# Attention with the values as stationary columns, one stream of scores in threes, and a hand-written order of side work

## The chip, the cores and the metric

The kernel runs on one NeuronCore of a Trainium2 chip. The core has five engines that run side by side and wait for each other by semaphores: TensorE (PE, matmuls; PEld is its weight load), VectorE (DVE), ScalarE (ACT, here the exponentials), GpSimd (POOL) and SyncE (SP, which issues the DMAs). The metric is the device time of one execution in microseconds, as the median of several runs. A profile is one further execution, whose span goes from its first to its last instruction.

## What is computed

Two branches on the same `x` (2048 tokens, 448 features, bf16), mixed by a gate per token. Branch A is attention with 16 heads of 28 features; branch B is a filter in the frequency domain.

```python
qkv = (x @ wqkv).reshape(B, S, 3, H, Dh)...        # S = 2048, H = 16, Dh = 28
p = softmax(einsum("bhqd,bhkd->bhqk", q, k) * Dh ** -0.5)
a = einsum("bhqk,bhkd->bhqd", p, v)...  @ wo
X = rfft2(x) * (w_r + 1j * w_i)
b = irfft2(X)
g = sigmoid((x * gate_w).sum(-1, keepdims=True))
out = g * a + (1 - g) * b
```

The Fourier transforms are matmuls with constant matrices, in several stages: along the features (f1), then along the tokens in two steps (stage A, and f34, which also multiplies by the filter), then back (stage A again as f5, and f678).

## The kernel before

**Head.** `phase_setup` loads `x` as one DMA, transposes it on TensorE (64 transposes, L257) into `xT`, and prepares weights. `proj_setup`, `proj_matmuls` (L353), `proj_knorm` and `proj_qbias` build q and k for head 15 (copied to three row groups by DMA, L359) and for the first four heads; `vproj_and_gate` (L290) makes all values `vsb`, with a column of ones beside each head, and the gate. Then the main loop starts.

**Softmax without a maximum.** Each query and key carries one extra row, so that a score comes out with a bound subtracted: half the squared query norm and half the largest squared key norm. The exponential can then follow the scores directly.

**Main loop.** `main_loop_group` takes heads in groups: first head 15 alone with three query blocks of 512 (and then its fourth block alone, the 16 narrow exponentials), then five groups of three heads. For each block of 128 keys it computes three score tiles of 128 keys by 512 queries in row groups of the array (L553), one exponential over the three (L557, `Pt`), and twelve small matmuls (L562) in which 128 columns of `Pt` are the weights and the 29 columns of `vsb` move. `psPV` collects queries on partitions, so the denominator is a column: after 16 key blocks VectorE takes the reciprocal of 12 columns (L568) and multiplies three times into `osb` (L571).

**Side work.** The projections of the other heads (`proj_tile`) and the Fourier stages (L603 to L718) are written after the groups with a lower priority; the scheduler of the framework places them where engines have room. They share one PSUM buffer, `ps_bg`; the scores have two buffers of three banks each, and `psPV` has one. `tail` transposes `osb`, multiplies by `wo` (L747), applies gate and branch B (L749) and stores (L751).

Of the kernel before, what the change touches and what calls it, by code (L numbers as in the profile page):

```python
# [17 lines left out]
BG_PRIORITY_BASE = 10_000_000  # L18


def bcast_last(ap: bass.AP, n: int) -> bass.AP:
    assert ap.ap[-1][1] == 1
    new_ap = [list(p) for p in ap.ap[:-1]] + [[0, n]]
    return bass.AP(tensor=ap.tensor, offset=ap.offset, ap=new_ap)


def strided_rows(t_ap: bass.AP, row0: int, stride: int, count: int) -> bass.AP:
    pstep = t_ap.ap[0][0]
    return _AP(tensor=t_ap.tensor, offset=t_ap.offset + row0 * pstep,
               ap=[[pstep * stride, count]] + [list(x) for x in t_ap.ap[1:]])  # L30


def chunks_of(n: int, c: int):
    return [(i, min(c, n - i)) for i in range(0, n, c)]


def fft_consts(S: int, D: int):
    NT = S // 128
    P = 128
    J = P // NT  # L40
    F = D // 2 + 1
    F2 = 2 * F
    bf16 = ml_dtypes.bfloat16
    fch = chunks_of(F, 128)
# [4 lines left out]
    dch = chunks_of(D, 128)  # L49
    Bd_pad = np.zeros((len(dch) * 128, F2))  # L50
    Bd_pad[:D] = Bd
    c["Bd"] = np.ascontiguousarray(Bd_pad.reshape(len(dch), 128, F2).transpose(1, 0, 2))
# [3 lines left out]
    Es = np.sin(2 * np.pi * pp * bb / P)  # L56
    def perm(M):
        return np.ascontiguousarray(M.reshape(P, J, NT).transpose(0, 2, 1).reshape(P, P))
# [34 lines left out]
    Binv = np.zeros((P, 2 * len(fch), D))  # L93
    qi = 0
    for B in (Br, Bi):
        for (fs, fn) in fch:
            Binv[:fn, qi, :] = B[fs:fs + fn, :]
            qi += 1
    c["Binv"] = Binv
    return {k: v.astype(np.float32).astype(bf16) for k, v in c.items()}  # L100


class Kernel:
    def __init__(self, tc, A_x, A_wqkv, A_wo, B_w_r, B_w_i, gate_w, out):
        self.tc = tc
        nc = self.nc = tc.nc
        self.A_x, self.A_wqkv, self.A_wo = A_x, A_wqkv, A_wo
        self.B_w_r, self.B_w_i, self.gate_w, self.out_ap = B_w_r, B_w_i, gate_w, out
        self.H = H = 16
        self.S = S = A_x.shape[1]  # L110
        self.D = D = A_x.shape[2]
        self.Dh = Dh = D // H
        self.SCALE = float(Dh) ** -0.5
        self.NT = NT = S // 128
        self.P = P = 128
        self.J = P // NT
        self.F = F = D // 2 + 1
        self.F2 = 2 * F
        self.dch = chunks_of(D, 128)
        self.NDC = len(self.dch)  # L120
        self.fch = chunks_of(F, 128)
        self.QW = 512
        assert Dh + 1 <= 32 and S % 512 == 0 and P % NT == 0 and NT <= P and H % 4 == 0
        self.x = A_x[0]
        self.outv = out[0].rearrange("(p t) d -> p t d", t=NT)
        self.tiles = [[(s, 4 * T + s) for s in range(4)] for T in range(H // 4)]
        lastT = len(self.tiles) - 1
        hl = H - 1
        self.tiles[lastT] = [(s, h) for (s, h) in self.tiles[lastT] if h != hl]
        self.tiles.append([(0, hl)])  # L130
        self.repT = len(self.tiles) - 1
        self.head_loc = {}
        for T, ent in enumerate(self.tiles[:-1]):
            for s, h in ent:
                self.head_loc[h] = (T, s)
        groups = [("rep", hl)]
        others = [h for h in range(H) if h != hl]
        for i in range(0, len(others), 3):
            groups.append(("tri", others[i:i + 3]))
        self.groups = groups  # L140
        self.NG = len(groups)
        self._bgcount = 0
        self._bg_saved = None
        self._evac_cnt = 0

    def bg_begin(self):
        assert self._bg_saved is None
        self._bg_saved = self.tc.cur_priority
        self.tc.cur_priority = BG_PRIORITY_BASE + self._bgcount

    def bg_end(self):
        assert self._bg_saved is not None
        self._bgcount = self.tc.cur_priority - BG_PRIORITY_BASE
        self.tc.cur_priority = self._bg_saved
        self._bg_saved = None

    def setup_pools(self, ctx):
        tc = self.tc
        self.per = ctx.enter_context(tc.tile_pool(name="per", bufs=1))
        self.rot2 = ctx.enter_context(tc.tile_pool(name="rot2", bufs=2))  # L160
        self.rot3 = ctx.enter_context(tc.tile_pool(name="rot3", bufs=3))
        self.ps = ctx.enter_context(tc.tile_pool(name="ps", bufs=2, space=bass.MemoryType.PSUM))
# [10 lines left out]
    def evac2(self, o, i):  # L173
        if self._evac_cnt % 2 == 0:
            self.nc.vector.tensor_copy(out=o, in_=i)
        else:
            self.nc.scalar.copy(out=o, in_=i)
        self._evac_cnt += 1

    def build(self):  # L180
        with ExitStack() as ctx:
            self.setup_pools(ctx)
            self.phase_setup()
            self.fft_setup()
            NTL = len(self.tiles)
            self.qTt = [None] * NTL
            self.kTt = [None] * NTL
            def full_proj(Tlist):
                for T in Tlist:
                    self.proj_setup(T)  # L190
                for which in ("q", "k"):
                    for T in Tlist:
                        self.proj_matmuls(T, which)
                for T in Tlist:
                    self.proj_knorm(T)
                for T in Tlist:
                    self.proj_qbias(T)
            full_proj([self.repT, 0])
            self.vproj_and_gate()
            bg_items = [("proj", T) for T in range(1, NTL - 1)]  # L200
            bg_items += [("fft", f) for f in
                         [self.fft_f1, self.fft_f2, self.fft_f34, self.fft_f5, self.fft_f678]]
            npj = NTL - 2
            plan = {0: [0, npj], 1: [1, npj + 1], 2: [2, npj + 2], 3: [npj + 3], 4: [npj + 4]}
            issued = set()
            for g in range(self.NG):
                self.main_loop_group(g)
                self.bg_begin()
                for idx in plan.get(g, []):
                    if idx < len(bg_items) and idx not in issued:  # L210
                        kind, arg = bg_items[idx]
                        if kind == "proj":
                            self.proj_tile(arg, bg=True)
                        else:
                            arg()
                        issued.add(idx)
                self.bg_end()
            self.bg_begin()
            for idx in range(len(bg_items)):
                if idx not in issued:  # L220
                    kind, arg = bg_items[idx]
                    if kind == "proj":
                        self.proj_tile(arg, bg=True)
                    else:
                        arg()
                    issued.add(idx)
            self.tail()
            self.bg_end()

    def phase_setup(self):  # L230
        nc = self.nc
        P, NT, D, S, NDC, H, Dh = self.P, self.NT, self.D, self.S, self.NDC, self.H, self.Dh
        per = self.per
        dch = self.dch
        self.xtok = per.tile([P, NT, D], BF16, name="xtok", tag="xtok_osb")
        nc.sync.dma_start(out=self.xtok[:], in_=self.x.rearrange("(p t) d -> p t d", t=NT))
        self.ident = per.tile([P, P], BF16, name="ident")
        make_identity(nc, self.ident[:])
        W3 = 3 * D + 1
        self.Wqkv_sb = per.tile([P, NDC, W3], BF16, name="Wqkv_sb")  # L240
        self.Wo_sb = per.tile([P, NDC, D], BF16, name="Wo_sb")
        for c, (d0, dsz) in enumerate(dch):
            nc.sync.dma_start(out=self.Wqkv_sb[0:dsz, c, 0:3 * D], in_=self.A_wqkv[d0:d0 + dsz, :])
        for c, (d0, dsz) in enumerate(dch):
            nc.sync.dma_start(out=self.Wqkv_sb[0:dsz, c, 3 * D:3 * D + 1],
                              in_=self.gate_w[d0:d0 + dsz].rearrange("(d o) -> d o", o=1))
        for c, (d0, dsz) in enumerate(dch):
            nc.sync.dma_start(out=self.Wo_sb[0:dsz, c, :], in_=self.A_wo[d0:d0 + dsz, :])
        self.xT = per.tile([P, NDC, S], BF16, name="xT")
        TB = 12  # L250
# [550 lines left out]
```

## Time and profile before

| | us |
|---|---|
| three runs | 572.0, 582.96, 583.14 |
| median | 582.96 |
| span of the profiled execution | 564.9 |
| first wide exponential starts | 56.8 |
| last exponential ends | 545.4 |

```profile
## 2 busy tenths in 40 slices
PE   2979988999998899999899999999998998899986
...
ACT  2153986999999899999899999999999999999961
...
PEclk9989985699999575799575555757799589999996
```

The page divides the span into 40 equal slices, and each digit is the busy share of a slice in tenths. PEclk is the clock that TensorE was granted, in tenths of full speed. After the first four slices TensorE and ScalarE are both busy for nearly all of the span; the clock changes between about 5 and 9. A group of instructions is given with its line, engine, shapes, count, busy time and mean duration, and then the idle time of its engine just before it with what ended it. In a table of stretches, the columns behind the five engines' busy times are granted clock, DMA share and GB/s.

### The profile page before, as it was taken

To read this page: it belongs to the slowest core of one execution; us is meant where nothing else is said; L and a number is where in the kernel's file an instruction comes from. 1 tells how busy PE (TensorE), PEld (TensorE's weight loads), DVE (VectorE), ACT (ScalarE), POOL (GpSimd) and SP (SyncE) were. 2 spreads that over 40 slices of the span, in tenths; PEclk is the share of its full clock that TensorE was granted. 3 is DMA by queue.
4 is the path that set the end of the run, shared out by engine and by line. 5 is a ranking of instruction groups with operands and counts; after the bars stand their busy time and mean duration, and the time that the engine had idled before them with its cause. 6 is when DMAs were issued, how large, how long until landed. Compare 5 with 4: busy or idle time off the path is not lost.

```text
span 564.9 us, 13975 instructions
## 1 busy us (share of the span) xinstructions
PE 508.8 (90%) x6088; PEld 256.5 (45%) x6088; DVE 213.8 (38%) x633; ACT 490.0 (87%) x392; POOL 20.8 (4%) x92
## 2 busy tenths in 40 slices
PE   2979988999998899999899999999998998899986
PEld 2424432444443355544355555555544554445541
DVE  4573323322223533322556555333233233333343
ACT  2153986999999899999899999999999999999961
POOL 6240010000000000000000000000000000000000
PEclk9989985699999575799575555757799589999996
DMA  7300000000000000000012221000000000000111
GB/s 252 126 19 20 2 2 1 2 1 2 2 1 2 3 1 1 1 3 1 1 33 54 55 55 26 1 2 1 20 21 20 21 20 20 21 1 27 34 34 41
DMA packets 13947, 13.45 MB, mean 24 GB/s; under 512 B 6191, under 2 KB 12783, under 8 KB 13758
## 3 DMA queue, kind: packets, MB, share of 16 engines
q1 hardware_dynamic: 13886, 12.57, 7.8%
q8 instruction: 47, 0.77, 0.6%
q14 instruction: 14, 0.11, 0.1%
HBM read 10.14 MB, written 1.84 MB: 21 GB/s over the span
## 4 chain that ended last, share of the span: by engine, by line
ACT 48%; PE 39%; issue 7%; DVE 3%; DMA 1%; SPq 0%; ACTq 0%
ACT Pt L557 48%; PE psS L553 12%; PE psPV L562 9%; PE pv L290 2%; PE pqk L353 2%; PE psT L641 2%; DMA Wqkv_sb<-in_A_wqkv_dram 1%; PE psY L714 1%; PE pf_s L747 1%; PE ptx L257 1%; PE psB L662 1%; PE psA L623 1%; PE psZ L705 1%; DVE fin L749 1%; PE psB L664 1%
## 5 line engine op out<-in xcount | busy, mean ns | idle before, releaser
L557 ACT ACTIVATE Pt<-psS 128x1536 bf16<-128x1536 f32 (+1 forms) x352 | 469.4, 1460 | 19.4 <-PE psS L553 10.2
L562 PEld LDWEIGHTS <-Pt 128*128 128x128 bf16 x4096 | 142.3, 100 | 131.1 <-ACT Pt L557 109.6
L562 PE MATMUL psPV<-vsb,Pt 128*128 128x29 bf16 x4096 | 167.1, 182 | 25.3 <-ACT Pt L557 20.8
L553 PE MATMUL psS<-qTa_2343,kTa_2344 32*128 32x512 bf16 x256 | 69.3, 507 | 0.5 <-ACT Pt L557 0.5
L553 PE MATMUL psS<-qTa_950,kTa_951 32*128 32x512 bf16 x256 | 68.8, 530 | 0.4 <-ACT Pt L557 0.4
L553 PE MATMUL psS<-qTa_249,kTa_250 32*128 32x512 bf16 x256 | 60.6, 439 | 1.8 <-ACT Pt L557 1.8
L553 PE MATMUL psS<-qTa_3760,kTa_3761 32*128 32x512 bf16 x192 | 26.5, 384 | 0.5 <-ACT Pt L557 0.4
L718 DVE TENSOR_SCALAR bm_sb<-psY,omg 128x448 bf16<-128x448 f32 x16 | 10.9, 683 | 36.8 <-PE psY L714 36.8
L667 DVE CAST Xri<-psB 128x225 bf16<-128x225 f32 x16 | 6.3, 396 | 25.7 <-PE psB L665 25.7
L749 DVE SCALAR_TENSOR_TENSOR fin<-pf,gsb,bm_sb 128x448 bf16<-128x448 f32 x12 | 8.2, 684 | 20.7 <-PE pf L747 20.7
L257 PE MATMUL ptx<-ident,xtok 128*128 128x128 bf16 (+1 forms) x64 | 6.7, 287 | 10.3 <-DMA xtok<-in_A_x_dram 7.7
L553 PEld LDWEIGHTS <-kTa_250 32*128 32x128 bf16 x256 | 12.8, 93 | 6.4 <-issue 2.3
L747 PE MATMUL pf<-Wo_sb,oTt 128*128 128x448 bf16 (+1 forms) x48 | 14.8, 374 | 0.7 <-DVE oTt L740 0.7
L553 PE MATMUL psS<-qTa_207,kTa_208 32*128 32x512 bf16 x64 | 14.4, 420 | 0.6 <-ACT Pt L557 0.5
L553 PEld LDWEIGHTS <-kTa_951 32*128 32x128 bf16 x256 | 13.0, 97 | 4.1 <-issue 1.8
L553 PEld LDWEIGHTS <-kTa_2344 32*128 32x128 bf16 x256 | 13.0, 95 | 3.6 <-issue 1.2
L571 DVE TENSOR_TENSOR osb<-psPV,recip 128x112 bf16<-128x112 f32 x64 | 13.6, 266 | 0.6
L290 PE MATMUL pv<-Wqkv_sb,xT 128*128 128x449 bf16 x64 | 13.5, 372 | 0.0
L603 DVE CAST V_5523<-psA 97x256 bf16<-97x256 f32 x16 | 6.8, 424 | 16.4 <-PE psA L625 16.4
L603 DVE CAST U_192<-psA 128x256 bf16<-128x256 f32 x16 | 6.8, 425 | 15.7 <-PE psA L625 15.7
L623 PE MATMUL psA<-R_sb,X_sb 128*128 128x256 bf16 (+1 forms) x32 | 12.2, 383 | 0.0
L623 PE MATMUL psA<-R_sb,G_sb 128*128 128x256 bf16 (+1 forms) x32 | 12.2, 382 | 0.0
(484 smaller groups left out, 541.6 us busy)
## 6 DMA issues: line engine op xcount, KB each, us to landing
RBg<-cRB SPq DMA_DIRECT2D x16, 128.0 KB, 2.0
xtok<-in_A_x_dram SPq DMA_DIRECT2D x1, 1792.0 KB
out_dram<-fin SPq DMA_DIRECT2D x16, 112.0 KB, 1.7
CSg<-cCS SPq DMA_DIRECT2D x16, 96.0 KB, 1.8
Wqkv_sb<-in_A_wqkv_dram SPq DMA_DIRECT2D x3, 336.0 KB, 7.4
Wg<-in_B_w_r_dram SPq DMA_DIRECT2D x16, 56.2 KB, 1.8
Wg<-in_B_w_i_dram SPq DMA_DIRECT2D x16, 56.2 KB, 2.0
Bd_sb<-cBd SPq DMA_DIRECT2D x1, 450.0 KB, 3.8
```

The source lines that it names most:

```text
L257: nc.tensor.transpose(out=pt[0:dsz, k, :], in_=self.xtok[:, t, d0:d0 + dsz], identity=self.ident[:])
L290: nc.tensor.matmul(pv[:, e, 0:D + 1], lhsT=self.xT[:, c, 128 * t:128 * t + 128], rhs=self.Wqkv_sb[:, c, 2 * D:3 * D + 1], start=(c == 0), ...
L353: nc.tensor.matmul(pqk[0:M, e, :], lhsT=Wg[:, c, 0:M], rhs=self.xT[:, c, 512 * b:512 * b + 512], start=(c == 0), stop=(c == NDC - 1))
L553: nc.tensor.matmul(psS[:, e, :], lhsT=kTa[32 * s:32 * s + 32, 128 * i:128 * i + 128], rhs=qTa[32 * s:32 * s + 32, qs:qs + QW], start=True, ...
L557: nc.scalar.activation(out=Pt[:, 0:ne, :], in_=psS[:, 0:ne, :], func=ACT.Exp, scale=self.SCALE)
L562: nc.tensor.matmul(psPV[:, e, j, 0:Dh + 1], lhsT=Pt[:, e, 128 * j:128 * j + 128], rhs=self.vsb[:, i, h, 0:Dh + 1], start=first, stop=last)
L571: nc.vector.tensor_tensor(out=self.osb[:, t0:t0 + NQT, h * Dh:(h + 1) * Dh], in0=psPV[:, e, :, 0:Dh], in1=bcast_last(recip[:, e, :, 0:1], Dh),
L603: self.nc.vector.tensor_copy(out=o, in_=i)
L623: nc.tensor.matmul(ps[0:fn, :], lhsT=data_sb[:, t, fs:fs + fn], rhs=Rr, start=True, stop=False)
L641: nc.tensor.transpose(out=psT[:, ri * 256 + fs:ri * 256 + fs + fn], in_=U_tiles[fb][0:fn, ri, g, :], identity=self.ident[0:fn, 0:fn])
L747: nc.tensor.matmul(pf[:, 0:D], lhsT=oTt[0:dsz, c, :], rhs=self.Wo_sb[0:dsz, c, :], start=(c == 0), stop=(c == NDC - 1))
L749: nc.vector.scalar_tensor_tensor(out=fin[:], in0=pf[:, 0:D], scalar=self.gsb[:, t:t + 1], in1=self.bm_sb[:, t, :], op0=ALU.mult, op1=ALU.add)
```

## The change

The file is written anew; what follows is its core, with `...` for what is left out. Shapes are now constants at the top of the file (P = 128, QW = 512, NT = 16, NTH = 4 groups of four heads, NQ = 4 query blocks, DH = 28, NC_ = 4 feature chunks of CK = 112).

Every instruction goes through a wrapper that keeps it in the order in which the program issues it on its engine; priorities and the scheduler's choice are gone:

```diff
+class InOrder:
+    ...
+    def __getattr__(self, name):
+        f = getattr(self._eng, name)
+        return lambda *a, **k: self._tc.keep_in_program_order(f(*a, **k))
```

The scores of all heads form one stream: chunks are (group of four heads, query block), and blocks (chunk, key block, head) are taken three at a time, across chunk borders. Values are column-tiled: 32 columns of `vsb` are the weights at column group `s`, and 512 columns of the exponential move, so `psPV` now has features on partitions, four heads below each other, with the denominator in row 28 of each 32.

```diff
-                    for j in range(NQT):
-                        last = (i == NKT - 1) and (e == ne - 1) and (j == NQT - 1)
-                        nc.tensor.matmul(psPV[:, e, j, 0:Dh + 1],
-                                         lhsT=Pt[:, e, 128 * j:128 * j + 128],
-                                         rhs=self.vsb[:, i, h, 0:Dh + 1],
-                                         start=first, stop=last)
...
+        chunks = [(T, q) for T in range(NTH) for q in range(NQ)]
+        seq = [(ci, i, s) for ci in range(len(chunks)) for i in range(NT) for s in range(4)]
+        steps = [seq[m:m + 3] for m in range(0, len(seq), 3)]
...
+        def values():
+            while pending:
+                pt, e, (ci, i, s) = pending.pop(0)
+                T, q = chunks[ci]
+                if i == 0 and s == 0:
+                    self.psPV = self.ps_pv([P, QW], F32, name="psPV")
+                nc.tensor.matmul(self.psPV[32 * s:32 * s + 32, :],
+                                 lhsT=self.vsb[:, i, 4 * T + s, :], rhs=pt[:, e, :],
+                                 start=(i == 0), stop=(i == NT - 1), tile_position=(0, 32 * s))
+                if i == NT - 1 and s == 3:
+                    self.normalise(T, q, self.psPV)
+                    if T == NTH - 1:
+                        last = q == NQ - 1
+                        ts = range(4 * q, 4 * q + 4)
+                        if last:
+                            for t in ts:
+                                self.out_tile(t, True)
+                        else:
+                            self.units += [None] * 4 + [lambda t=t: self.out_tile(t, False) for t in ts]
+                    return
...
+        scores(0)
+        self.v_tile(0)
+        self.v_tile(1)
+        for m in range(n + 1):
+            if m < n:
+                exps(m)
+            if m + 1 < n:
+                scores(m + 1)
+            if m > 0:
+                pending += [(Pt[m - 1], e, x) for e, x in enumerate(steps[m - 1])]
+            values()
+            if m == n:
+                while pending:
+                    values()
+            elif self.units:
+                u = self.units.pop(0)
+                if u is not None:
+                    u()
```

So each step issues one exponential, the scores of the next step, the values of the step before, and one unit of side work. A unit is one PSUM tile of side work: its matmuls and its evacuation by VectorE. `plan` lists them: 14 V tiles mixed with 6 units of queries, the gate, 16 units for the projection of each further group of heads (a unit of four matmuls, and one of one or two for norms), and the Fourier stages; all use `ps_bg`, still one buffer.

```diff
+        u += self.proj_units(1)
+        u += self.f1_units()
+        u += self.stage_A_units(lambda: (self.X1, self.U), 0)
+        f34, f678 = self.f34_units(), self.f678_units()
+        u += self.before(lambda: self.f34_load(0), self.proj_units(2))
+        u += f34
+        u += self.proj_units(3)
+        u += self.before(lambda: self.f678_load(0), self.stage_A_units(self.f5_open, 2))
+        u += f678
```

At the end of a chunk the denominators are rows, and are spread by DMA before the reciprocal; the product lies as weights for the last projection, whose 64 transposes and copies are gone (`WoP` has the rows of `wo` in the same places):

```diff
-            nc.vector.reciprocal(out=recip[:, 0:ne, :, :], in_=psPV[:, 0:ne, :, Dh:Dh + 1])
...
+    def normalise(self, T, q, psPV):
+        nc = self.nc
+        oU = self.rot2.tile([P, QW], F32, name="oU")
+        nc.vector.tensor_copy(out=oU[:], in_=psPV[:])
+        rB = self.rot2.tile([P, QW], F32, name="rB")
+        for s in range(4):
+            nc.sync.dma_start(out=rB[32 * s:32 * s + 32, :],
+                              in_=row_times(oU[:, :], 32 * s + DH, 32))
+        nc.vector.reciprocal(out=rB[:], in_=rB[:])
+        nc.gpsimd.tensor_tensor(out=self.oT[T][:, QW * q:QW * q + QW], in0=oU[:], in1=rB[:],
+                                op=ALU.mult)
+
+    def out_tile(self, t, last):
+        ...
+        for T in range(NTH):
+            nc.tensor.matmul(pf[:, 0:D], lhsT=self.oT[T][:, P * t:P * t + P], rhs=self.WoP[:, T, :],
+                             start=(T == 0), stop=(T == NTH - 1))
+        fin = self.rot2.tile([P, D], BF16, name="fin")
+        nc.vector.scalar_tensor_tensor(out=fin[:], in0=pf[:, 0:D], scalar=self.gsb[:, t:t + 1],
+                                       in1=self.bm[t // 4][:, t % 4, :], op0=ALU.mult, op1=ALU.add)
+        nc.sync.dma_start(out=self.outv[:, t, :], in_=fin[:])
```

In the order of VectorE's instructions the reciprocal stands directly behind the copy to `oU`, ahead of the evacuation of the unit of the same step.

`x` comes in four pieces (the first, then the q and k weights of the first four heads, then the others), and `head` transposes and projects piece by piece, for four heads' keys and the first 512 queries only; the squared norms are summed by matmuls with a constant matrix `sel`. The values and the other queries are units of the first steps. No head is replicated any more.

```diff
+        tposes(0)
+        tposes(1)
+        keys(0)
+        ...
+        tposes(2)
+        norms(0)
+        ...
+        keys(1)
+        tposes(3)
+        norms(1)
+        keys(2)
+        norms(2)
+        keys(3)
+        norms(3)
+        nc.vector.tensor_reduce(out=self.nhk[0][:], in_=self.nm[0][:], axis=AX.X, op=ALU.min)
+        nc.vector.tensor_scalar(out=self.qT[0][:, 0:QW], in0=pq[:],
+                                scalar1=self.nhk[0][:, 0:1], scalar2=None, op0=ALU.add)
```

The features are cut into four chunks of 112 instead of 128, 128, 128 and 64. The evacuations of the f34 and f678 stages are one copy where there were two, and the loads of their constants are issued one unit pair ahead, with three buffers instead of two.

## The prediction

> **What bounds the kernel now.** I read the page first, then the ScalarE groups by form, the chain of waits in order of time, the timeline of single steps, and the stretches with their clocks.
>
> ```profile
> PE 508.8 (90%) x6088; PEld 256.5 (45%) x6088; DVE 213.8 (38%) x633; ACT 490.0 (87%) x392; POOL 20.8 (4%) x92
> ...
> ACT 48%; PE 39%; issue 7%; DVE 3%; DMA 1%; SPq 0%; ACTq 0%
> ```
>
> ScalarE (ACT) and TensorE (PE) are both nearly full, and the chain of waits runs through both. The next view separates the shapes of the exponential; the one after it gives the pace.
>
> ```profile
> L557 ACT ACTIVATE Pt<-psS 128x1536 bf16<-128x1536 f32 x336 | 460.2, 1500 | 16.4 <-PE psPV L562 7.9 <-PE psS L553 7.5 <-PE pn_3826 L493 0.4
> L557 ACT ACTIVATE Pt<-psS 128x512 bf16<-128x512 f32 x16 | 9.6, 609 | 2.9 <-PE psS L553 2.7 <-PE psPV L562 0.2
> ```
> ```profile
> 142.15 1.22 ACT Pt L557
> 143.48 1.23 ACT Pt L557
> 144.81 1.25 ACT Pt L557
> ```
>
> One wide exponential lasts 1.50 us, but neighbours overlap: they start 1.33 us apart. So 336 x 1.33 + 16 x 0.55 = 456 us is ScalarE's floor. The first exponential starts at 56.8 and the last ends at 545.4, which is 489 us: 33 us are lost to waits. Before it lie 56.8 us of head, after it 19.5 us of tail: 56.8 + 456 + 33 + 19.5 = 565, the span. The median run, 583.0, stands 18.1 us above this span; I add 18 to every span below.
>
> TensorE per step, at full clock and (last two lines) at half clock:
>
> ```profile
> 142.52 0.46 PE L562 MATMUL psPV<-vsb,Pt 128*128 128x29 bf16 x12 [0.26 <-ACT Pt L557]
> 142.92 0.39 PE L553 MATMUL psS<-qTa_249,kTa_250 32*128 32x512 bf16 x3
> ...
> 218.57 0.60 PE L553 MATMUL psS<-qTa_249,kTa_250 32*128 32x512 bf16 x1
> ...
> 219.11 0.39 PE L623 MATMUL psA<-R_sb,X_sb 128*128 128x256 bf16 x1
> ```
>
> Three row-tiled score matmuls overlap fully: 0.39 us for three, next work 0.32 us after their start; at half clock 0.54.
>
> **Head.** Today's 56.8 us become: the first quarter of x and the small weights landed by about 4 us (the whole of x is there at 7.7 us today); 64 transposes, 16 in 1.89 us, 7.5 us; 20 projection matmuls of 512 columns, 4.6 us at the 0.23 us of L353; six matmuls for norms and bias, 2.4 us; then a closing chain of Square 0.6, norm 0.4, reduce 0.68, a tiny reduce 0.15, q bias 0.74, scores 0.4, about 3.5 us with hand-overs. Sum 22, plus 3 for evacuations that do not fit: 25 (21 to 31). Saves 32.
>
> **Exponentials.** 1024 score blocks in threes are 341 wide and one narrow: 341 x 1.33 + 0.55 = 454. Saves 2.
>
> **The values matmul.** 4096 matmuls of 29 columns, each loading 128 exponential columns, become 1024 of 512 columns in column tiles. No row shows a column tile. Bound from below: three overlap as three row tiles do, next work after 0.32 us, a little less than the 0.40 of today's twelve; from above: they run one behind the other, 3 x 0.22 + 0.1 = 0.75. I take 0.32, since row tiles are the nearest row. A step then costs TensorE 0.64 plus its unit.
>
> The Trainium skill ("TensorE: Matmul & The Clock Gate", Part 3) measured three column tiles 2.38 times as fast as one by one; "TensorEngine Tiling (Array Packing)", Key Properties, speaks against the change: switching tiling mode drains the array, and a step now switches three times. By the first, 3 x 0.22 / 2.38 = 0.28 us, an estimate; no run shows either yet.
>
> **One unit per step, one bank.** Units use a single PSUM buffer ("bg"), so unit plus evacuation must fit in 1.33. A first-FFT or V unit: 4 matmuls 0.76, pipe 0.17, evacuation 0.63 (X_sb 128x450), hand-over 0.1 = 1.66, V 0.15 more for the gate column; projection pairs average (1.86 + 1.30)/2 = 1.58. Excess 16 x 0.33 + 14 x 0.48 + 54 x 0.25 = 25 us if nothing hides it, 8 if only TensorE's own time counts: 20, with about 1 us at each of three projections for GpSimd's eight weight copies (0.2 to 0.33 each, L458). Other units fit.
>
> **Edits with one answer.** The 64 output transposes and their 64 copies vanish with the new layout of the projection weights; they lay beside exponentials, except in the tail. The remaining loads stand on SP behind x; the V weights are needed from about 26 us and land in some 8 (336 KB took 7.4 today), so they cost nothing unless the queue is 10 us late.
>
> **The end of a chunk.** This is where I see the decision. Today normalising is one reciprocal of 12 columns and three multiplies. After the change, VectorE (DVE) copies psPV to oU, four DMAs spread each head's denominator over 32 partitions, VectorE takes the reciprocal of 128x512, GpSimd multiplies. The instruction order keeps that reciprocal ahead of every later evacuation on VectorE.
>
> ```profile
> L568 DVE RECIPROCAL recip<-psPV 128x12 f32<-128x12 f32 x21 | 4.8, 231 | 13.3 <-PE psPV L562 13.3
> ...
> L568 DVE RECIPROCAL recip<-psPV 128x4 f32<-128x4 f32 x1 | 0.2, 182 | 0.3 <-PE psPV L562 0.3
> ...
> L299 DVE RECIPROCAL gsb<-ge 128x16 f32<-128x16 f32 x1 | 0.3, 253 | 0.0
> ...
> L298 DVE TENSOR_SCALAR ge<-ge 128x16 f32<-128x16 f32 x1 | 0.2, 163 | 0.0
> ```
>
> From 4 to 12 columns the reciprocal grows by 49 ns, 6.2 ns a column; at 16 columns it is 90 ns over an ordinary operation. So 512 columns: 0.18 + 508 x 0.0062 = 3.3 us. From below it is 0.69, like any f32 pass of 512 (qTa 128x512).
>
> ```profile
> kTa_208<-kTa_208 SPq DMA_DIRECT2D x2, 128.0 KB, 2.8
> ...
> qTa_207<-brow SPq DMA_DIRECT2D x1, 4.0 KB, 1.7
> ```
>
> These SBUF-to-SBUF copies land in 1.7 to 2.8 us, and SP needs 0.43 to 0.59 us to issue each; four of 64 KB: 3 x 0.5 + 2.4 = 4.0 with the hand-over (3.2 to 4.6).
>
> Time from the end of the exponential before the chunk's last values: scores and values done 0.8, oU 1.5, DMAs 5.5, reciprocal 8.8, the held evacuation 9.3. TensorE executed that unit, and is stopped at the next unit, which needs the bank; the scores for three steps on are queued behind it. Unit 0.3 to 0.9, scores 0.4: exponential m+3 starts at about 10.2. Exponentials m to m+2 had their scores, so ScalarE is out of work at 3 x 1.33 = 4.0. Stall 6.2 us. The 245 units (14 V, 6 q, gate, 3 x 16 projection, 16 + 32 + 32 + 32 + 64 FFT) last for the first 245 of 342 steps, in which 11 chunks end: 68 us. Chunk 11 ends without units. After the next three, four empty steps precede the output tiles, which need GpSimd's product (no row for it; between the 0.53 and 1.8 us of its memsets, 1.1) at 9.9 and are reached at 6.1: 3 to 8 us each, 15.
>
> SP's own queue adds nothing: its loads ahead of the four DMAs wait for buffers freed a unit earlier.
>
> **The clock.** A TensorE that stands still for 7 us loses its clock:
>
> ```profile
> 180.00:184.00 4.00, 2.41 (x33) 1.11 (x33) 2.69 (x7) 2.89 (x3) 0.00 (x0) 1.00 0.02 4
> 184.00:188.00 4.00, 3.00 (x32) 1.09 (x31) 3.18 (x6) 1.70 (x2) 0.00 (x0) 0.50 0.00 0
> 300.00:345.00 45.00, 43.90 (x546) 25.85 (x547) 25.26 (x118) 42.19 (x32) 0.00 (x0) 0.50 0.23 54
> ```
>
> The third number from the right is the granted clock: a gap around 181 is followed by 0.50, and from 300 to 345 it stays at 0.50 although PE is busy 43.90 of 45. At 0.50 a step costs 1.08 plus its unit: 0.40 for stage A (still 1.48), about 0.7 for the inverse FFT, 1.3 to 1.6 for projection and first FFT. With some 10 slow steps of 0.25 us excess after each of 11 stalls: 27 us (8 to 50), 25 taken. Steps without a unit fit under 1.33 even then.
>
> The same page of the skill (Part 1) says one sustained busy window of about 3.4 us restores the full clock; the 45 us above contradict it. By the rule only three steps would be slow, 11 x 0.75 = 8 us, and the sum 17 lower.
>
> **Tail.** Values 0.45, oU 0.7, DMAs 4, reciprocal 3.3, product 1.1, four tiles at 1 to 1.76 (L747), 0.68, output 2: 18 (16 to 20) for 19.5.
>
> **Sum.** 25 + 454 + 20 + 68 + 15 + 25 + 18 = 625 us span, 643 as a run: the head's 32 us are won, and waits grow from 33 to 128.
>
> **Rivals.** A, faster: the normalisation is covered, since the reciprocal streams at f32 speed (0.69) and the DMAs land in 2.5. The stall is DMA + reciprocal - 1.1 us, so 2.1 a chunk, 23 in all, with 5 of clock and the output steps free: 25 + 454 + 20 + 23 + 5 + 17 = 544, 562 as a run. For it: only tiny reciprocals are in the trace. Against: three sizes on one line. It decides if stall and clock together cost under 3.2 us a chunk (35/11, from 536 without any).
> B, the column tiles do not overlap: 0.43 us more per step. Light steps hide it; stage A is 0.05 over, inverse FFT 0.18, forward 0.12, projection 0.4, V and first FFT 0.6: 3 + 11 + 4 + 19 + 18 = 55 more, 698. Against: row tiles overlap.
> C, the stalls stand but the clock returns at once and slow units hide: 25 + 454 + 8 + 68 + 9 + 8 + 17 = 589, 607.
>
> **Numbers.** Forecast 0.67, A 0.14, B 0.10, C 0.09. The forecast's own range is 610 to 675; the range 588 to 688 takes in C and the upper end without B. A measurement here tells about 2% from no change: faster under 571, slower over 595. From A 0.11 faster; 0.07 within; 0.82 slower.
>
> **What would show it.** RECIPROCAL at 128x512 near 3.3 us, 16 times; VectorE held about 7 us before an evacuation at 11 chunk ends; ScalarE gaps of about 6 us there, waiting for scores; the clock at 0.50 after each; the first exponential near 25. A reciprocal near 0.7, gaps under 2 us, or values matmuls three in 0.75 would prove me wrong.

## The result, and the profile after

The changed kernel takes 761 us (median of four runs, 758 to 770) against 583 for the kernel before. Executions of the kernel before fall into a faster group (564 to 574 us over all series) and a slower one (582 to 591), and every ratio to it compares the faster ones alone: here 1.33, 95% interval 1.319 to 1.341. The direction was forecast, the size was not: 643 us, with a range of 588 to 688. The profiled execution ran 759.0 us and its span is 757.3.

From the page of the changed kernel: the busy times, the slices of ScalarE and of TensorE's granted clock, and the chain of waits.

```profile
PE 516.0 (68%) x2928; PEld 161.8 (21%) x2928; DVE 241.4 (32%) x431; ACT 486.6 (64%) x357; POOL 58.2 (8%) x76
...
ACT  3388285593845928459385692937759975949370
...
PEclk9599698795566958779655585975856556565655
...
PE 39%; DVE 19%; DMA 16%; ACT 14%; issue 9%; SPq 3%; POOL 1%; POOLq 0%; DVEq 0%; ACTq 0%
```

ScalarE does the same work as before (486.6 us against 490.0) but is busy 64% of the span, not 87. Its slices show deep holes at regular distances, one at each chunk end, and the chain has moved: ScalarE's share fell from 48% to 14%, VectorE and DMA hold 35% where they held 4.

The table of waits (us in total, times, longest) says who is late, and the groups and DMA rows of the page what each piece costs:

```profile
ACT Pt L109 <- PE psS L109: 226.3, 153, 14.1
DVE rB L109 <- DMA rB<-oU: 149.2, 16, 10.4
```
```profile
L109 ACT ACTIVATE Pt<-psS 128x1536 bf16<-128x1536 f32 x342 | 477.4, 1499 | 227.5 <-PE psS L109 226.3
...
L109 DVE RECIPROCAL rB<-rB 128x512 f32<-128x512 f32 x16 | 53.6, 3353 | 149.2 <-DMA rB<-oU 149.2
L109 POOL TENSOR_TENSOR oT<-oU,rB 128x512 bf16<-128x512 f32 x16 | 20.2, 1262 | 543.1 <-DVE rB L109 543.1
...
rB<-oU SPq DMA_DIRECT2D x64, 64.0 KB, 7.2
```

The reciprocal takes 3.353 us, as forecast (3.3). But VectorE stands 149.2/16 = 9.3 us before each one, waiting for the four transfers, where my sum had 4.0; one transfer takes 7.2 us from issue to landing.

The timeline of one chunk end (start, duration, engine; in brackets the idle time before it and who ended it), weight loads left out:

```profile
166.84 0.39 PE L109 MATMUL psS<-qT,kT 32*128 32x512 bf16 x3 [0.30 <-ACT Pt L109]
...
167.17 0.40 PE L109 MATMUL psPV<-Pt,vsb 128*32 128x512 bf16 x3
...
167.49 0.42 PE L109 MATMUL psA<-R,X 128*97 128x256 bf16 x2
167.61 0.69 DVE L109 COPY oU<-psPV 128x512 f32<-128x512 f32 x1 [0.60 <-PE psPV L109]
...
168.37 3.19 SPq L109 DMA_DIRECT2D rB<-oU  x4
...
177.61 3.35 DVE L109 RECIPROCAL rB<-rB 128x512 f32<-128x512 f32 x1 [9.30 <-DMA rB<-oU]
180.88 0.36 DVE L109 CAST U<-psA 97x256 bf16<-97x256 f32 x1
...
181.29 0.58 PE L109 MATMUL psA<-R,X 128*128 128x256 bf16 x2 [12.38 <-DVE U L109]
181.81 0.61 PE L109 MATMUL psS<-qT,kT 32*128 32x512 bf16 x3
182.34 0.61 PE L109 MATMUL psPV<-Pt,vsb 128*32 128x512 bf16 x3
182.52 1.45 ACT L109 ACTIVATE Pt<-psS 128x1536 bf16<-128x1536 f32 x1 [11.70 <-PE psS L109]
```

The unit's matmuls (psA) end at 167.9; their evacuation (CAST U) stands behind the reciprocal and runs at 180.88, so the next unit has no bank and the scores behind it are not issued for 12.38 us. That is the mechanism as forecast, but nearly twice as long: ScalarE is out of work for 11.70 us here, where my sum had 6.2. Two more things are to be seen. Before the stall three values matmuls take 0.40 us and the next work starts 0.32 after theirs: the column tiles overlap. After it the same matmuls take 0.61: TensorE's clock is down.

The windows (length, busy time and count of PE, PEld, DVE, ACT and POOL, then clock, DMA share, GB/s) show how long it stays down:

```profile
160.00:170.00 10.00, 7.07 (x54) 2.83 (x54) 3.13 (x7) 10.00 (x9) 0.00 (x0) 1.00 0.04 2
170.00:180.00 10.00, 0.00 (x0) 0.00 (x0) 2.39 (x1) 0.82 (x1) 0.00 (x0) 0.63 0.56 45
180.00:190.00 10.00, 8.71 (x42) 2.16 (x41) 3.36 (x7) 6.67 (x5) 3.04 (x9) 0.50 0.01 2
190.00:200.00 10.00, 10.00 (x49) 2.39 (x48) 2.55 (x6) 8.78 (x7) 0.00 (x0) 0.50 0.00 0
200.00:210.00 10.00, 10.00 (x52) 2.45 (x51) 2.55 (x6) 8.78 (x7) 0.00 (x0) 0.50 0.00 0
```

In the second window the DMA engines are 0.56 busy and move 45 GB/s; at the start of the kernel they move 232 GB/s at 0.9. So the amount moved does not look like what limits the transfers; the experiments test that.

### The profile page after: what moved, and what is told of

Its sections match the earlier page's. It is cut to its first block, busy times and chain, and to the rows that moved or that the text cites. A ratio compares the mean times of both kernels' runs of the same rounds, so it can differ in the third digit from the quotient of the medians.

```text
span 757.3 us, 7514 instructions
## 1 busy us (share of the span) xinstructions
PE 516.0 (68%) x2928; PEld 161.8 (21%) x2928; DVE 241.4 (32%) x431; ACT 486.6 (64%) x357; POOL 58.2 (8%) x76
## 4 chain that ended last, share of the span: by engine, by line
PE 39%; DVE 19%; DMA 16%; ACT 14%; issue 9%; SPq 3%; POOL 1%; POOLq 0%; DVEq 0%; ACTq 0%
DMA rB<-oU 15%; ACT Pt L109 13%; PE psS L109 8%; PE psPV L109 8%; DVE rB L109 5%; PE psA L109 4%; PE pq L109 3%; SPq L109 3%; PE pvp L109 2%; PE psx L109 2%; DVE cm_t L109 2%; PE pkb L109 2%; PE psY L109 2%; DVE qT L109 2%; PE pf L109 2%
## 5 line engine op out<-in xcount | busy, mean ns | idle before, releaser
L109 ACT ACTIVATE Pt<-psS 128x1536 bf16<-128x1536 f32 x342 | 477.4, 1499 | 227.5 <-PE psS L109 226.3
L109 PE MATMUL psS<-qT,kT 32*128 32x512 bf16 x1024 | 172.3, 494 | 28.7 <-ACT Pt L109 26.6
L109 PE MATMUL psPV<-Pt,vsb 128*32 128x512 bf16 x1024 | 175.2, 499 | 2.6 <-DVE oU L109 1.4
L109 DVE RECIPROCAL rB<-rB 128x512 f32<-128x512 f32 x16 | 53.6, 3353 | 149.2 <-DMA rB<-oU 149.2
L109 PEld LDWEIGHTS <-kT 32*128 32x128 bf16 x1024 | 44.6, 95 | 150.1 <-issue 143.1
L109 POOL TENSOR_TENSOR oT<-oU,rB 128x512 bf16<-128x512 f32 x16 | 20.2, 1262 | 543.1 <-DVE rB L109 543.1
L109 PEld LDWEIGHTS <-vsb 128*32 128x32 bf16 x1024 | 36.1, 97 | 117.5 <-issue 115.3
L109 PE MATMUL psA<-R,G 128*128 128x256 bf16 (+1 forms) x64 | 19.8, 411 | 24.6 <-DVE V L109 24.4
L109 PE MATMUL psY<-Binv,ZT 128*128 128x448 bf16 x64 | 20.1, 451 | 12.4 <-DVE ZT L109 12.4
L109 PE MATMUL psA<-R,X 128*128 128x256 bf16 (+1 forms) x64 | 17.6, 370 | 12.4 <-DVE U L109 12.4
L109 DVE TENSOR_SCALAR bm<-psY,omg 128x448 bf16<-128x448 f32 x16 | 10.8, 677 | 26.1 <-PE psY L109 26.1
```

The costliest lines, as they stand in the source:

```text
L109: return lambda *a, **k: self._tc.keep_in_program_order(f(*a, **k))
```

## The experiments

All kernels start from the changed one. Where one time is given, it is that of a single run; the kernel before took 564 to 591 us in the runs beside them. "Gap" is the time between the starts of two exponentials (1.33 when ScalarE is the bound).

**Without the spread (e1_no_spread).**

```diff
-        for s in range(4):
-            nc.sync.dma_start(out=rB[32 * s:32 * s + 32, :],
-                              in_=row_times(oU[:, :], 32 * s + DH, 32))
-        nc.vector.reciprocal(out=rB[:], in_=rB[:])
+        nc.vector.reciprocal(out=rB[:], in_=oU[:])
```

> Leaves out the four transfers that spread the denominators; the reciprocal is taken of oU itself, so every value is divided by itself (and vsb holds ones in all four spare columns, so that no division is by zero). Theory D, the transfers' wait is the term I sized wrongly (9.3 us of VectorE waiting per chunk in the trace, 4.0 in my sum): the ScalarE gap at the 11 chunk ends with units falls from 13.3-15.5 us to about 4.5, the three gaps before output tiles from 10.8-12 to about 2, the tail shrinks by 9; 11 x 9.3 + 3 x 9.5 + 9.3 = 140 us, and 10 to 20 us of clock with it: 600 to 620 us. Rival U, the loss is spread over the units (one bank, low clock) and the chunk-end gaps only show where it is booked: above 690 us.

619.1 us. From its page and table of waits:

```profile
L109 DVE RECIPROCAL rB<-oU 128x512 f32<-128x512 f32 x16 | 53.7, 3353 | 0.5
```
```profile
ACT Pt L109 <- PE psS L109: 94.1, 157, 4.8
```

The 140 us are the transfers' wait. By the starts of the exponentials the gap at the 11 chunk ends falls from 13.9 us on average to 4.5: 9.4 each, close to VectorE's wait of 9.3. The gaps before the output tiles fall from 10.8-12.0 to 2.4. With the tail, 9.2 shorter, this is nearly all of the 140; the 10 to 20 us of clock that were expected with it did not come.

**What makes a transfer slow (e2_own_rows, e10_other_rows).** Amount, number and row length stay; only the rows that are read change.

```diff
-                              in_=row_times(oU[:, :], 32 * s + DH, 32))
+                              in_=oU[32 * s:32 * s + 32, :])
```

> The same four transfers with the same bytes and the same 2 KB rows, but every destination row reads the row of its own partition (oU rows 32s to 32s+31) and not 32 times the row 32s+28; the division is by the value itself. Theory P, the 32 reads of one partition are what is slow: time to landing falls from 7.2 us to 2.8-3.5, VectorE's wait from 9.3 to about 5 per chunk, the run from 759 to about 690 (675 to 700). Rival Q, it is the amount (256 KB in 2 KB rows): 7.2 us to landing stay, and 750 to 765 us.

684.3 us. From its page (KB each, us to landing) and its waits:

```profile
rB<-oU SPq DMA_DIRECT2D x64, 64.0 KB, 2.0
```
```profile
DVE rB L109 <- DMA rB<-oU: 65.4, 16, 4.8
```

Landing falls from 7.2 us to 2.0, and VectorE's wait to 65.4/16 = 4.1 us, just what my sum had. But every row of e2 also stays in its own partition, so leaving the partition was a rival. In e10 the rows come from another head:

```diff
-                              in_=row_times(oU[:, :], 32 * s + DH, 32))
+                              in_=oU[32 * (3 - s):32 * (3 - s) + 32, :])
```

> As e2_own_rows, but each destination row reads a row of another head: rows 32s to 32s+31 of rB from rows 32(3-s) to 32(3-s)+31 of oU, so every row is read once and leaves its partition. The division is by another value. Theory P, what is slow is that 32 packets read one partition: landing stays near e2_own_rows' 2.0 us (2.0 to 3), the run at 680 to 690. Rival X, what is slow is leaving the partition: landing back near 7.2 us and the run near 759.

679.4 us, and its row reads the same:

```profile
rB<-oU SPq DMA_DIRECT2D x64, 64.0 KB, 2.0
```

So the price is that of many packets reading one partition. In the packet records of one chunk end the 128 packets of 2 KB took 602 ns in the median in the changed kernel, and 145 in e2 and e10; the fastest 81 to 84 in all three. In each of the three up to 16 packets are under way at once, so it is not that fewer packets of the changed kernel move side by side.

**Reciprocal later (e4_defer).** The computation is unchanged; `later` runs ahead of a step's unit.

```diff
-        nc.vector.reciprocal(out=rB[:], in_=rB[:])
-        nc.gpsimd.tensor_tensor(...)
+        def piece(j):
+            c = slice(PC * j, PC * j + PC)          # PC = 128
+            nc.vector.reciprocal(out=rB[:, c], in_=rB[:, c])
+            nc.gpsimd.tensor_tensor(out=self.oT[T][:, QW * q + PC * j:QW * q + PC * j + PC],
+                                    in0=oU[:, c], in1=rB[:, c], op=ALU.mult)
+        ...
+            self.later += [(self.m + 9 + j, lambda j=j: piece(j)) for j in range(4)]
...
-                            self.units += [None] * 4 + [...]
+                            self.units += [None] * 14 + [...]
```

> The transfers stay; the reciprocal and the product are cut into four pieces of 128 columns, which stand in the order 9 to 12 steps later, ahead of those steps' units; output tiles 10 steps later. Theory B, all of the loss at a chunk end is evacuations held behind a reciprocal that waits: the gaps of 12 to 15 us vanish, the clock stays higher, and the run takes 31 + 454 + about 50 for one-bank units and pieces + 24 tail = 560 us (545 to 580), under the kernel before. Rival N, a new wait takes its place (pieces of about 1 us in front of evacuations, PSUM's one bank for values): over 600.

567.3 us, 194 less than the changed kernel, as theory B expected. This one run lies among those of the kernel before (564 to 591), so it shows no gain over that kernel. Slices of the clock, and waits:

```profile
PEclk9969999999999995669999997999955556556576
```
```profile
ACT Pt L109 <- PE psS L109: 48.7, 79, 4.5
```

The transfers still take 7.3 us, but no evacuation waits behind them, and the clock holds nearly everywhere up to the steps without units (from 407 us on). One large gap was left, 6.0 us behind a chunk end in the forward Fourier stage, where TensorE waits for the constants CSg. Of their 16 loads the slowest lands in 6.2 us, the median in 2.0; the one waited for was issued at 240.40, directly behind the four transfers in SyncE's queue.

**TensorE kept at work through the stall (e6_warm, e7_warm52).**

```diff
                     self.normalise(T, q, self.psPV)
+                    if self.units:
+                        dm = self.ps_pv([P, QW], F32, name="dummy")
+                        for k in range(40):          # e7_warm52: 52
+                            nc.tensor.matmul(dm[:], lhsT=self.ident, rhs=self.qT[0][:, 0:QW],
+                                             start=True, stop=True)
```

> After each of the 11 chunk ends that still have units, 40 matmuls of 512 columns with results that nobody reads are put between the normalisation and the held unit: about 9 us of TensorE work inside a stall of 12 us, so the wait itself stays as long. Theory K, the low clock after a stall is a price of its own (steps of 1.6 to 2.9 us in place of 1.33 after the gap, 0.50 held into later steps): the run falls by 25 to 45 us to 715-735. Rival: the steps are paced by the one bank, not by the clock: 752 to 765; above 770 if the 40 matmuls don't fit in the stall.

755.7 us: no gain, so by the numbers the rival. But the timeline of the same chunk end showed that the premise had failed:

```profile
163.99 8.34 PE L109 MATMUL dummy<-qT,IS 128*128 128x512 bf16 x35
...
174.83 0.38 PE L109 MATMUL psA<-R,X 128*128 128x256 bf16 x2 [1.63 <-DVE U L109]
...
175.46 0.61 PE L109 MATMUL psPV<-Pt,vsb 128*32 128x512 bf16 x3
```

A standstill of 1.63 us was left (1.1 to 3.2 behind the eleven chunk ends), and 0.6 us after it ended the matmuls run at half clock again. The second try fills it.

> As e6_warm, with 52 matmuls in place of 40, so that no gap of 1.6 us is left at the end of the wait (e6_warm came to 755.7 with the clock at 0.50 again from 175 us on, 0.7 us after that gap). Theory K2, the clock falls by the standstill itself: without one it stays at 1.00 after most chunk ends, the steps behind them take 1.33 in place of 1.65, and the run is 720 to 738. Rival, the clock falls whenever the exponentials resume, or the slow steps are paced by the bank: 750 to 765.

720.2 us, 39 us of span less than the changed kernel, with stalls nearly as long as before: the eleven gaps are 13.4 us on average, where they were 13.9. One line of its timeline, and the windows:

```profile
163.67 11.38 PE L109 MATMUL dummy<-qT,IS 128*128 128x512 bf16 x52 [0.79 <-DVE oU L109]
```

```profile
160.00:170.00 10.00, 8.64 (x49) 3.85 (x47) 1.54 (x3) 4.79 (x4) 0.00 (x0) 1.00 0.44 22
170.00:180.00 10.00, 9.30 (x58) 3.87 (x57) 4.91 (x6) 4.06 (x3) 3.06 (x9) 1.00 0.17 27
180.00:190.00 10.00, 7.76 (x62) 3.09 (x61) 3.40 (x8) 10.00 (x9) 0.00 (x0) 1.00 0.00 0
190.00:200.00 10.00, 8.02 (x64) 3.17 (x61) 2.98 (x7) 10.00 (x8) 0.00 (x0) 1.00 0.01 2
```

The stall is there (ScalarE 4.79 and 4.06 of 10), but the clock stays at 1.00, and behind it ScalarE is full (10.00) where it was 8.78. With 40 matmuls the run was no faster, with 52 it was: the low clock is a price of its own. A standstill of 1.6 us can be enough to bring it, but does not always: in e6 the clock fell behind nine of the eleven, while one of 2.75 us at 129.5 left it at 1.00; in e7 it fell behind one of the eleven chunk ends, after a standstill of 1.46 us.

**Without division (e5_no_division).** What is left without any wait at a chunk end:

```diff
-        rB = self.rot2.tile([P, QW], F32, name="rB")
-        (four transfers, reciprocal, product)
+        nc.gpsimd.tensor_copy(out=self.oT[T][:, QW * q:QW * q + QW], in_=oU[:])
```

> Leaves out the division: no spread, no reciprocal, GpSimd only copies oU into oT. What is left between 31 + 454 us and the end is units, clock and tail. Theory W, the units at one step each with one bank lose more than the 20 us of my sum (with the clock 47): the trace of the changed kernel shows 54 us lost outside the chunk ends, 14 of them at the V units; then 31 + 454 + 50 + 12 tail = 547 (538 to 558). Rival, my term was right and the excess there is only an echo of the stalls: 31 + 454 + 20 + 12 = 517 (510 to 528).

542.4 us. Slices of the clock, and waits:

```profile
PEclk9859999999999999979999999999985558576677
```
```profile
ACT Pt L109 <- PE psS L109: 34.2, 80, 3.2
```

Nothing holds an evacuation back, the clock is full nearly everywhere up to the steps without units, and still the gaps sum to 47 us over 341 x 1.33. By the gaps 38 of them lie in steps with units, 8 at output tiles, and 1 in the other steps: theory W. The difference to e1, 617.4 - 540.6 = 77 us of span, is about what the reciprocal in the wrong place costs with its clock.

**A faster kernel (e8_defer_tail, e9_small_pieces).** e8 is e4 with the last chunk's spread done by a matmul and the loads of the forward Fourier stage issued two groups ahead:

```diff
+        def last_piece(j):
+            c = slice(PC * j, PC * j + PC)
+            nc.vector.reciprocal(out=rc[:, c], in_=psPV[:, c])     # rc: bf16
+            nc.tensor.matmul(rep[:, c], lhsT=self.rep, rhs=rc[:, c], start=True, stop=True)
+            nc.vector.tensor_tensor(out=self.oT[T][...], in0=rep[:, c], in1=oU[:, c], op=ALU.mult)
...
-                load(g + 1)
+                load(g + 2)
```

> e4_defer (567 us) with two edits more: after the last chunk the denominators are spread by a matmul with a constant 0/1 matrix from reciprocals of 128 columns, each followed by its output tile, in place of transfers of 9 us and a reciprocal of 3.4; and the loads of the forward FFT's middle stage are issued two groups ahead, since e4_defer waits 6 us there for CSg. The tail falls from 21 to about 11 and the FFT wait goes: 551 us (545 to 558), 0.94 of before. Rival, the tail is bound by the output tiles and their writes: 558 to 568.

560.6 us (median of four), ratio to before 0.981 (0.967 to 0.995); the profiled execution took 556.2. The rival was nearer. By its trace the tail fell only from 21.3 to 17.7 us, since on VectorE the evacuation of each output tile stood ahead of the next reciprocal, and two waits for loads were left (start, duration, idle before):

```profile
212.08 0.93 PE L112 MATMUL psB<-UT,CSg 128*128 128x225 bf16 x4 [2.23 <-DMA CSg<-cCS]
```
```profile
338.76 0.58 PE L112 MATMUL psZ<-RBg,VT 128*128 128x256 bf16 x2 [2.52 <-DMA RBg<-cRB]
```

Issuing the CSg loads earlier helped only in part (the longest wait for them was 4.2 us in e4): with three buffers a load waits for the buffer that an earlier group still reads, and the one waited for here stands directly behind the four transfers in SyncE's queue (they are issued from 201.66 on, it at 204.95). The RBg loads were still issued one group ahead. e9 gives both stages four buffers, cuts the pieces to 64 columns in eight steps, and evacuates the last tiles later:

```diff
-            CS = self.rot3.tile([P, 3, P], BF16, name="CSg")
+            CS = self.rot4.tile([P, 3, P], BF16, name="CSg")
...
-        PC = 128
+        PC = 128 if end else 64
...
-            self.later += [(self.m + 9 + j, lambda j=j: piece(j)) for j in range(4)]
+            self.later += [(self.m + 8 + j, lambda j=j: piece(j)) for j in range(8)]
```

> e8_defer_tail (profiled at 556) with the pieces of reciprocal and product cut to 64 columns over eight steps, the loads of both FFT stages issued two groups ahead into four buffers in place of three (e8 waits 2.2 us for CSg and 2.5 us for RBg, each followed by the clock at 0.50), and the last four output tiles no longer behind each other's evacuation. Expected: tail from 18 to about 12, 8 us less in the FFT steps: 543 us (536 to 550), 0.95 of before. Rival: the pieces are not what the FFT steps wait for, and the loads neither: 550 to 558, not told from before by 2 per cent.

548.2 us (median of six, 546 to 549): 0.965 of the kernel before, 95% interval 0.958 to 0.972, and 0.72 of the changed one by the medians. The tail is 14.4 us, where 12 was expected. From its page:

```profile
PE 449.9 (82%) x2932; PEld 161.6 (30%) x2932; DVE 245.7 (45%) x542; ACT 478.2 (88%) x358; POOL 76.0 (14%) x180
...
PEclk9759999999999999979999999999975555858577
...
L112 ACT ACTIVATE Pt<-psS 128x1536 bf16<-128x1536 f32 x342 | 468.4, 1647 | 35.5 <-PE psS L112 35.4
```

ScalarE is busy 88% again, and waits 35 us where the changed kernel waited 227. Which of e9's edits gave how much was not tried one by one.

## Why the prediction had the direction and missed the size

Read from the exponentials' starts, the 757 us of span divide as follows; e7 and e5 give the two rows that one trace alone does not part.

| Term | On record | Measured | From |
|---|---|---|---|
| Head, to the first exponential | 25 | 31 | start at 31.1 |
| Exponentials | 454 | 454 | 1.33 us between starts |
| Stalls at 11 chunk ends | 68 | 139 | the 11 gaps, less 1.33 each |
| Before the output tiles | 15 | 30 | three gaps of 12.0, 10.8, 10.8, less 1.33 each |
| Clock | 25 | 39 | spans of the changed kernel and e7 |
| Units with one bank | 20 | 38 | e5 |
| Tail | 18 | 24 | last exponential starts at 733.1 |
| Sum | 625 | 755 | |

The rows for the clock and the units are approximate, since they come from other runs: 7 of the 39 are shorter stalls and output gaps in e7, which stand in the rows above as well, and the 9 us of e5 outside the steps with units stand in no row. In the changed kernel's own gaps the two come to 80 us together.

**The step that failed is the price of the four transfers**: "four of 64 KB: 3 x 0.5 + 2.4 = 4.0 with the hand-over (3.2 to 4.6)". I took it from SBUF-to-SBUF copies that read many partitions, and the sum fitted those: with such sources e2 waits 4.1 us. The transfers of the change read one partition 32 times each, and the wait is 9.3. The missing 5.3 us stand in three terms: 11 x 5.3 = 58 of the 71 missing at chunk ends, all 15 before the output tiles (3 x 5.3 = 16), and 5 in the tail, 78 of 130. The range went wrong with it: I bounded this term by rows of another access pattern and called the upper end 4.6.

**The rest of the stall** is 1.2 us per chunk (13 in all). Part of it is that I resumed at full clock, while the first unit and scores after the standstill run at half (0.58 and 0.61 in the timeline): in e7, mostly at full clock there, the gaps are 0.5 us shorter. What the other 0.7 is was not tried.

**Head**: 31 for 25. My sum had its 20 projection matmuls at full clock, 4.6 us. Four of their five groups of four took 1.9 us each, about the time of half clock, where the fifth took 1.03; together they took 8.7, which is 4 of the 6 us.

**Clock**: right in kind, 39 for 25, inside my 8 to 50. Stage A at half clock takes 1.65 us a step, not the 1.48 of my sum. The Trainium skill ("TensorE: Matmul & The Clock Gate", Part 1) says that a busy window of about 3.4 us brings the full clock back, and an idle window of that length takes it away. The windows from 190 to 210 above, 10.00 busy of 10 at 0.50 (as the profile models a matmul's end), speak against the first half; e6 against the second, where the clock fell after a standstill of 1.63 us. Rival C stood on the first half and is out.

**Units**: 38 for 20. In e5 the first three steps take 4.6, 2.5 and 2.4 us at the low clock of the head's end, the steps of the middle forward Fourier stage (f34) take 1.55 on average where I had written "Other units fit", and I had taken 5 off the full price (25) for hiding that did not come.

**Around the span**: "The median run, 583.0, stands 18.1 us above this span; I add 18". This was a mistake of its own. It set the span of one execution beside the time of others, and a run is its own span and little more: 759.0 against 757.3 here, 548.0 against 546.3 in e9. Only 2 of the 18 were due, so this error hid 16 us of the others.

**What held.** The reciprocal (3.35 for 3.3, from an extrapolation of 12 columns to 512), so rival A is out. The column tiles: next work 0.32 us after three of them, so rival B (0.75) is out. By 52 matmuls in 11.38 us one takes 0.219, and three in 0.32 are 2.05 times as fast as one by one; Part 3 of the same page measured 2.38. The drain at a switch of tiling mode ("TensorEngine Tiling (Array Packing)", Key Properties) can cost little here: 166.84, 167.17 and 167.49 are the starts of row tiles, column tiles and a full matmul, so each set of three takes about 0.1 us more than one such matmul (0.219), the switch included; no run parts it from the rest. And the place of the loss: e4 moves the reciprocal and the product, in pieces, and the output tiles behind them, and takes 194 us off.

## What to carry to other kernels

When an order of instructions is fixed by hand, whatever waits longest must not stand ahead of work that frees a resource: here the same reciprocal and product, ten steps later and in pieces, took 194 us off, and with changes to the tail and the loads as well (e9) the kernel is faster than before. Price a transfer by rows with its access pattern, not only its kind and size; where no row has it, the upper bound must be wide. And compare a prediction with the run that the profile belongs to, not with a median of other runs.

## What the runs showed of the hardware

- Four transfers that each read one partition's 2 KB row 32 times land in 7.2 us, and in 2.0 when each row is read once, from the own partition or from another head's. At one chunk end the median packet took 602 ns against 145.
- TensorE's granted clock fell to 0.50 at 175.5 us in e6, 0.7 us after a standstill of 1.63 us, although TensorE had just run matmuls for 8 us. Without that standstill (e7) it stayed at 1.00 there. This is no fixed rule: at 129.5 in e6 a standstill of 2.75 us left it at 1.00.
- At 0.50 it can stay while TensorE is busy 10.00 of 10 us (190 to 200 and 200 to 210): in the changed kernel it is low from 172.6 to 217.0, until two us before the next standstill. Why it comes back when it does was not settled.
- A reciprocal of 128 columns takes 930 ns and one of 64 columns 530, so 6.25 ns a column; with the 3353 for 512 columns (6.31 from 128 on) the slope that 4 to 12 columns showed holds throughout.
